# Seven of eight blocks of wo loaded as four neighbouring rows to a lane, with o rearranged to match

## The chip, the cores and the metric

The kernel runs on one core of one Trainium2 chip. The metric is the device time of one execution in microseconds. The core has a matrix engine (PE, with its weight loads shown apart as PEld), a vector engine (DVE), an activation engine (ACT), GpSimd (POOL), and SyncE (SP), which here issues nearly all transfers. Sixteen DMA engines move data between the chip's memory (HBM) and the on-chip memory SBUF; matmuls write to PSUM.

## The reference, cut to what matters

A decode step: four sequences with one token each, width 640, and two branches added to the residual.

```
xn  = layernorm(x)                                # 4 x 640
q   = (xn @ wq)  -> 4 x 32 heads x 128
p   = softmax(q k^T / sqrt(128))                  # over 4096 cached positions
o   = p v        -> 4 x 32 x 128
out = x + o.reshape(4, 4096) @ wo + gmlp(xn)      # wo is 4096 x 640
```

The caches k and v are 4 x 32 x 4096 x 128 in bf16, 128 MiB each. There is one query per head, so every byte of the caches is used once. wo is 4096 x 640 in bf16, 5 MiB. The output is rounded to bf16.

## The kernel before, in words

**Tiles.** The work is cut into NT = 32 steps. Step i is a group hg of HT = 4 heads and one sequence b: `hg, b = divmod(i, 4)`. A step needs one k tile and one v tile of 128 lanes x 16,384 elements, 4 MiB each. A lane holds 128 consecutive positions of one head, so 32 lanes belong to a head, and a lane's 32 KB are contiguous in HBM.

**Loads.** k and v tiles share five buffers (KV_SLOTS); the weights wq, w_in and w_out take three of them first. `pump()` issues the next load from SP (L121) as soon as the tile that held the buffer before has been used. The order is written out in `loads`; twice (EXTRA_K) two k tiles follow each other, and from then on the v part of a step runs one step further behind (`turns`). The last v tile is cut into pieces.

**wo.** There are eight blocks of 512 rows, one for each group of four heads, in one buffer (`wop`, one tile of 128 x 4 x 640). `load_wo(j)` is issued from SP (L155) at the end of step 4j + 2, behind the k and v loads issued by then; block 7 is issued after the loop in four pieces (L153). Row 128 hh + p of a block goes to lane p, part hh. So a lane gets four rows that lie 128 rows apart, 1,280 B each.

**A step.** The order of each engine's instructions is written out by hand. On DVE: the product of k with the query (L397, four quarters), a halving sum of each (L409), the rest of the sum over PE (`sums`, L421) and `row_sums` (L432), then `lane_max` (L441). The maximum is turned on PE (`turn_max`, L446), reduced per head on DVE (`head_max`, L451), spread over lanes on PE (`spread_max`, L462), and used in the exponentials on ACT (L474). These are done in the next step, between the first quarters of its products. `blocks` (L489) and `gather` (L506) form p v on PE, for the step that `turns` names.

**A group.** When the fourth sequence of a group has been through `blocks`, `group_den` sums the exponentials over lanes (L530) and takes the reciprocal (L534), and `group_norm` (L539) writes o_n: 128 lanes (the position in the head) x 4 heads x 4 sequences, bf16. `group_proj` (L548), in the next step after `turn_max`, multiplies it into `out_ps`: eight matmuls, one for each head and half of the 640 columns, with o_n of a head as weights and part hh of wo as moving data. `out_ps` gathers the residual, the gMLP branch and all groups, and is written out at the end.

**PSUM.** qbc_ps, den, mT and nb_ps rotate through one pool, `ps_m`, of two buffers.

Of the kernel before, what the change touches and what calls it, by code (L numbers as in the profile page):

```python
# [9 lines left out]
FP32 = mybir.dt.float32  # L10
BF16 = mybir.dt.bfloat16
ACT = mybir.ActivationFunctionType
ALU = mybir.AluOpType
AX = mybir.AxisListType
# [6 lines left out]
def kernel(  # L21
# [14 lines left out]
    nc = tc.nc  # L36
    P = nc.NUM_PARTITIONS
    Bsz, Sq, D = A_x.shape
# [9 lines left out]
    HT = 4  # L48
    HG = H // HT
    NT = HG * Bsz  # L50
    LN = P // HT
# [12 lines left out]
    const = ctx.enter_context(tc.tile_pool(name="const", bufs=1))  # L64
# [5 lines left out]
    small = ctx.enter_context(tc.tile_pool(name="small", bufs=2))  # L70
# [3 lines left out]
    ps_m = ctx.enter_context(tc.tile_pool(name="ps_m", bufs=2, space=PSUM))  # L74
# [13 lines left out]
    for c0, c1 in ((0, HT), (HT, DC)):  # L88
# [14 lines left out]
        out=w_out_sb[:, 0:NFF, :], in_=B_w_out[0 : NFF * P].rearrange("(p k) n -> p k n", k=NFF)  # L103
# [34 lines left out]
    def pump():  # L138
        while n_loaded[0] < len(loads):
            at = n_loaded[0] + 3 - KV_SLOTS  # L140
            if at >= 0 and occupants[at] not in used:
                return
            load(*loads[n_loaded[0]])
            n_loaded[0] += 1

    wo_v = A_wo.rearrange("(j h p) n -> j p h n", p=P, h=HT)
    wo_tiles = {}

    def load_wo(j):
        wo_tiles[j] = wop.tile([P, HT, D], BF16, name="wo")  # L150
        if j == HG - 1:
            for hh in range(HT):
                nc.sync.dma_start(out=wo_tiles[j][:, hh, :], in_=wo_v[j][:, hh, :])  # L153
            return
        nc.sync.dma_start(out=wo_tiles[j][:], in_=wo_v[j])  # L155

    pump()

# [2 lines left out]
    ident = const.tile([P, P], BF16)  # L161
# [19 lines left out]
        out=sel[:],  # L181
        in_=ident_f[:].rearrange("p (g q) -> p q g", g=CG)[:, 0 : GC * HT, :],
        axis=AX.X,
        op=ALU.add,
    )

    NACC = 2
# [10 lines left out]
    for i in range(NSTAT):  # L198
# [5 lines left out]
        out=rstd[:], in_=mv[:, 1:2], func=ACT.Sqrt, bias=eps_tile[:Bsz], scale=1.0  # L204
# [4 lines left out]
        out=xn_bf[:],  # L209
        in0=x_bf[:],  # L210
# [8 lines left out]
    for c in range(DC):  # L219
        nc.tensor.transpose(  # L220
            out=xnT_ps[:, c, :], in_=xn_v[:, c, :], identity=ident[:Bsz, :Bsz]
# [5 lines left out]
    for h in range(H):  # L227
        for c in range(DC):
            t, i = wq_parts[c]
            nc.tensor.matmul(  # L230
                out=q_ps[:, h, :],
                lhsT=t[:, i, h * Dh : (h + 1) * Dh],
                rhs=xnT[:, c, :],
                start=(c == 0),
                stop=(c == DC - 1),
# [9 lines left out]
    def out_sum(half):  # L245
        return out_ps[OG * half : OG * half + Bsz, :]

    for half in range(2):
        nc.tensor.matmul(
            out=out_sum(half),  # L250
            lhsT=ident[:Bsz, :Bsz],
            rhs=x_bf[:, half * NOH : (half + 1) * NOH],
            start=True,
            stop=False,
# [124 lines left out]
    def stage_q(i):  # L379
        hg, b = divmod(i, Bsz)  # L380
        qb_ps = ps_m.tile([P, Dh], FP32, tag="m", name="qbc_ps")
        for hh in range(HT):
            nc.tensor.matmul(  # L383
                out=qb_ps[hh * LN : (hh + 1) * LN, :],
                lhsT=qT[:, HT * hg + hh, b : b + 1].to_broadcast([P, LN]),
                rhs=ident[:],
                start=True,
                stop=True,
            )
        qbcs[i] = small.tile([P, Dh], BF16, name="qbc", bufs=3)  # L390
        nc.scalar.copy(out=qbcs[i][:], in_=qb_ps[:])  # L391
# [3 lines left out]
    def product(i, q):  # L395
        t = prods[i, q] = prod.tile([P, QC, Dh], BF16, name="prod")
        nc.vector.tensor_tensor(  # L397
            out=t[:],
            in0=k_tiles[i][:, q * QC : (q + 1) * QC, :],
            in1=qbcs[i][:, None, :].to_broadcast([P, QC, Dh]),  # L400
            op=ALU.mult,
        )

    def fold_half(i, q):
        t = prods.pop((i, q))
        half, part = divmod(q, 2)
        if part == 0:
            folds[i, half] = fold.tile([P, HC, HD2], BF16, name="folded")
        nc.vector.tensor_tensor(  # L409
            out=folds[i, half][:, part * QC : (part + 1) * QC, :],  # L410
            in0=t[:, :, 0:HD2],
            in1=t[:, :, HD2:Dh],
            op=ALU.add,
        )

    def sums(i, half):
        t = folds.pop((i, half))
        s = sums_ps[i, half] = ps_s.tile([P, HC, RW], FP32, name="s_ps")
        n = HD2 // RW
        for g in range(n):  # L420
            nc.tensor.matmul(  # L421
                out=s[:],
                lhsT=ident[:],
                rhs=t[:, :, g * RW : (g + 1) * RW],
                start=(g == 0),
                stop=(g == n - 1),
            )
# [72 lines left out]
    def gather(i, stop=True):  # L500
        hg, b = divmod(i, Bsz)
        if b == 0:
            pvs[hg] = ps_pv.tile([P, HT, Bsz], FP32, tag="pv", name="pv")
        pv_sb = blocks_sb.pop(i)
        for k in range(GC):
            nc.tensor.matmul(  # L506
                out=pvs[hg][:, :, b],
                lhsT=pv_sb[:, k * Dh : (k + 1) * Dh],
                rhs=sel[:, k * HT : (k + 1) * HT],
                start=(k == 0),  # L510
                stop=stop and k == GC - 1,
            )
# [13 lines left out]
    gr = {}  # L526
# [10 lines left out]
    def group_norm(hg):  # L537
# [3 lines left out]
        )  # L541
        gr[hg] = o_n

    def group_proj(hg):
        o_n = gr.pop(hg)
        for hh in range(HT):
            for half in range(2):
                nc.tensor.matmul(  # L548
                    out=out_sum(half),
                    lhsT=o_n[:, hh, :],  # L550
                    rhs=wo_tiles[hg][:, hh, half * NOH : (half + 1) * NOH],
                    start=False,
                    stop=(hg == HG - 1 and hh == HT - 1),
                )

    def group(i, fn):
        if 0 <= i < NT and i % Bsz == Bsz - 1:
            fn(i // Bsz)

    def at(i, fn, *args):  # L560
        if 0 <= i < NT:
            fn(i, *args)

    turns = {}
# [8 lines left out]
    with tc.manual_schedule(engines={E.PE, E.DVE, E.Activation, E.SP}):  # L573
        stage_q(0)
        stage_q(1)
        gmlp()
        used.update(occupants[:3])
        pump()
        for i in range(NT):
            j = turns.get(i)  # L580
            product(i, 0)
            fold_half(i, 0)
            at(i - 1, row_sums, 1)
            at(i - 1, lane_max)
            at(i - 1, turn_max)
            group(turns.get(i - 1, -1), group_proj)
            product(i, 1)
            at(i - 1, head_max)
            at(i - 1, spread_max)
            at(i - 1, exps)  # L590
            fold_half(i, 1)
            sums(i, 0)
            product(i, 2)
            if i + 2 < NT:
                stage_q(i + 2)
            fold_half(i, 2)
            due = [] if j is None else [j]
            if i == NT - 1:
                due += range(j + 1, NT - 2)
            for n, jj in enumerate(due):  # L600
                if n:
                    gather(due[n - 1])
                blocks(jj)
                group(jj, group_den)
                used.add(("v", jj))
            row_sums(i, 0)
            product(i, 3)
            fold_half(i, 3)
            if due:
                gather(due[-1])  # L610
            for jj in due:
                group(jj, group_norm)
            sums(i, 1)
            used.add(("k", i))
            pump()
            if i % Bsz == 2 and i // Bsz < HG - 1:
                load_wo(i // Bsz)
        load_wo(HG - 1)
        row_sums(NT - 1, 1)
        lane_max(NT - 1)  # L620
        turn_max(NT - 1)
        head_max(NT - 1)
        spread_max(NT - 1)
        exps(NT - 1)
        blocks(NT - 2)
        group_den(HG - 1)
        gather(NT - 2)
        blocks(NT - 1, 0, V_CUTS[1])
        gather(NT - 1, stop=False)
        for c0, c1 in zip(V_CUTS[1:], V_CUTS[2:]):  # L630
            pairs(NT - 1, c0, c1)
        group_norm(HG - 1)
        group_proj(HG - 1)

        res = work.tile([P, NOH], BF16, name="res")
        out_v = out.flatten_outer_dims()
        r0, r1 = slice(0, Bsz), slice(OG, OG + Bsz)
        nc.scalar.copy(out=res[r0], in_=out_ps[r0])
        nc.vector.tensor_copy(out=res[r1], in_=out_ps[r1])
        nc.scalar.dma_start(out=out_v[:, 0:NOH], in_=res[r0])  # L640
        nc.sync.dma_start(out=out_v[:, NOH:D], in_=res[r1])
# [30 lines left out]
```

## Time and profile before

| | |
|---|---|
| median of 3 runs | 670.0 us (669.78 to 670.29) |
| profiled execution | 669.68 us |
| its span, first to last instruction | 667.9 us |
| DVE busy | 506.7 us |
| PE busy | 347.9 us |
| moved by DMA | 282.63 MB in 14,663 packets, of which 5,548 are under 2 KB |
| wo, issue to landing (median of 7) | 44.7 us |
| k, issue to landing (median of 32) | 43.3 us |

The span is the part of the execution that the trace covers; the 1.8 us around it belong to the execution's own time. Busy time is per engine, and engines work beside each other. A DMA packet is one contiguous piece that one DMA engine moves; the time from issue to landing includes the time that a transfer stands in the queue behind others.

### The profile page before, as it was taken

What the parts mean: (1) busy time and instruction counts of PE and PEld (TensorE: products, weight loads), DVE (VectorE), ACT (ScalarE), POOL (GpSimd) and SP (SyncE); (2) the same over time, 40 slices, a digit from 0 to 9 for tenths busy, and PEclk for the clock granted to TensorE, in tenths of its full rate; (3) what the DMA queues carried; (4) which work ended last, traced back from release to release, by engine and by line L of the source; (5) the groups of instructions that cost most, each with busy time, mean ns of one, the idle gap of its engine ahead of it and who ended that gap; (6) DMA issues with size and microseconds to landing.
All of it is one profiled execution on the core that took longest, in us unless ns stands there. A gap on an engine that the chain in (4) does not pass through costs nothing.

```text
span 667.9 us, 5968 instructions
## 1 busy us (share of the span) xinstructions
PE 347.9 (52%) x2425; PEld 154.7 (23%) x2425; DVE 506.7 (76%) x435; ACT 113.0 (17%) x361; POOL 2.7 (0%) x13
## 2 busy tenths in 40 slices
PE   1627554535557345663346654455564556546575
PEld 0502221212222122221112221122222112222133
DVE  1299897867789677787777698776787899876961
ACT  0202111101111101111101111111111111110122
POOL 1000000000000000000000000000000000000000
PEclk9997766788766678775786866788766667786677
DMA  9999999999999999999999999999999999999996
GB/s 373 418 440 433 419 433 436 420 435 426 429 426 430 433 430 429 424 431 432 434 421 432 423 434 435 428 426 429 424 435 434 421 430 432 429 422 433 432 422 257
DMA packets 14663, 282.63 MB, mean 423 GB/s; under 512 B 1344, under 2 KB 5548, under 8 KB 5932
## 3 DMA queue, kind: packets, MB, share of 16 engines
q1 hardware_dynamic: 14616, 282.25, 99.1%
q8 instruction: 19, 0.31, 0.2%
q14 instruction: 8, 0.07, 0.0%
q10 hardware_dynamic: 20, 0.01, 0.0%
HBM read 282.24 MB, written 0.01 MB: 423 GB/s over the span
## 4 chain that ended last, share of the span: by engine, by line
DMA 68%; DVE 21%; PE 8%; SPq 1%; issue 1%; DVEq 0%
DMA k_nat<-in_A_k_cache_dram 63%; DVE prod L397 13%; PE s_ps L421 7%; DVE folded L409 5%; DMA v_nat<-in_A_v_cache_dram 5%; DVE s_sb L432 2%; PE pv_acc L489 1%; SPq L121 1%; DVE m L441 1%; DVE nm L451 0%; PE out_ps L548 0%; PE qbc_ps L383 0%; SPq L90 0%; SPq L102 0%; PE den L530 0%
## 5 line engine op out<-in xcount | busy, mean ns | idle before, releaser
L397 DVE TENSOR_TENSOR prod<-k_nat,qbc 128x4096 bf16<-128x4096 bf16 x128 | 292.7, 2287 | 91.4 <-DMA k_nat<-in_A_k_cache_dram 89.9
L421 PE MATMUL s_ps<-folded,ident 128*128 128x512 bf16 x512 | 186.9, 531 | 64.7 <-DVE folded L409 64.6
L409 DVE TENSOR_TENSOR folded<-prod 128x2048 bf16<-128x2048 bf16 x128 | 156.1, 1220 | 3.3
L421 PEld LDWEIGHTS <-ident 128*128 128x128 bf16 x512 | 64.9, 128 | 152.4 <-issue 135.3
L446 PE MATMUL mT<-ident_f,m 128*1 128x128 f32 x32 | 11.0, 344 | 154.8 <-DVE m L441 154.8
L474 ACT ACTIVATE pm<-s_sb,nb 32x128 bf16<-32x128 f32 x128 | 73.9, 578 | 2.6
L470 ACT COPY nb<-nb_ps 128x4 f32<-128x4 f32 x32 | 5.2, 162 | 394.9 <-PE nb_ps L462 394.9
L489 PE MATMUL pv_acc<-v_nat,pm 128*16 128x512 bf16 x1008 | 71.7, 434 | 0.2 <-DMA v_nat<-in_A_v_cache_dram 0.2
L432 DVE TENSOR_REDUCE s_sb<-s_ps 128x64 f32<-128x512 f32 x64 | 43.5, 680 | 7.8 <-PE s_ps L421 5.4
L462 PE MATMUL nb_ps<-nm,scale_row 1*128 1x4 f32 x64 | 18.2, 353 | 56.2 <-DVE nm L451 56.2
L506 PE MATMUL pv<-sel,pv_sb 128*128 128x4 f32 x256 | 34.4, 258 | 19.5 <-ACT pv_sb L497 19.5
L446 PEld LDWEIGHTS mT<-ident_f,m 128*1 128x1 f32 x32 | 2.5, 79 | 173.1 <-DVE m L441 141.8
L506 PEld LDWEIGHTS pv<-sel,pv_sb 128*128 128x128 f32 x256 | 31.6, 195 | 32.3 <-ACT pv_sb L497 32.3
L489 PEld LDWEIGHTS <-pm 128*16 128x16 bf16 x1008 | 26.6, 102 | 32.6 <-issue 17.2
L474 ACT ACTIVATION_READ_ACCUMULATOR pm<-s_sb,nb 32x1 f32 x128 | 32.2, 251 | 0.0
L462 PEld LDWEIGHTS nb_ps<-nm,scale_row 1*128 1x128 f32 x64 | 15.5, 299 | 66.7 <-DVE nm L451 59.8
L497 ACT COPY pv_sb<-pv_acc 128x512 f32<-128x512 f32 x32 | 18.7, 585 | 61.4 <-PE pv_acc L489 61.4
L391 ACT CAST qbc<-qbc_ps 128x128 bf16<-128x128 f32 x32 | 8.4, 265 | 80.0 <-PE qbc_ps L383 80.0
L534 DVE RECIPROCAL rden<-den 128x16 f32<-128x16 f32 x8 | 2.1, 258 | 21.9 <-PE den L530 21.9
L238 DVE CAST qT<-q_ps 128x128 bf16<-128x128 f32 x1 | 0.3, 292 | 15.1 <-PE q_ps L230 15.1
L230 PE MATMUL q_ps<-xnT,wq 128*128 128x4 bf16 x160 | 4.6, 167 | 10.5 <-DMA wq<-in_A_wq_dram 10.5
L441 DVE TENSOR_REDUCE m<-s_sb 128x1 f32<-128x128 f32 x32 | 9.2, 287 | 1.1
(76 smaller groups left out, 79.2 us busy)
## 6 DMA issues: line engine op xcount, KB each, us to landing
k_nat<-in_A_k_cache_dram SPq DMA_DIRECT2D x32, 4096.0 KB, 43.3
v_nat<-in_A_v_cache_dram SPq DMA_DIRECT2D x31, 4096.0 KB, 36.6
wo<-in_A_wo_dram SPq DMA_DIRECT2D x7, 640.0 KB, 44.7
wq<-in_A_wq_dram SPq DMA_DIRECT2D x1, 4096.0 KB, 12.7
w_sb<-in_B_w_in_dram SPq DMA_DIRECT2D x1, 2160.0 KB, 19.5
v_nat<-in_A_v_cache_dram SPq DMA_DIRECT2D x1, 2048.0 KB
wq<-in_A_wq_dram SPq DMA_DIRECT2D x1, 1024.0 KB, 14.8
v_nat<-in_A_v_cache_dram SPq DMA_DIRECT2D x1, 1024.0 KB
```

The costliest lines, as they stand in the source:

```text
L391: nc.scalar.copy(out=qbcs[i][:], in_=qb_ps[:])
L397: nc.vector.tensor_tensor(out=t[:], in0=k_tiles[i][:, q * QC : (q + 1) * QC, :], in1=qbcs[i][:, None, :].to_broadcast([P, QC, Dh]), op=ALU ...
L409: nc.vector.tensor_tensor(out=folds[i, half][:, part * QC : (part + 1) * QC, :], in0=t[:, :, 0:HD2], in1=t[:, :, HD2:Dh], op=ALU.add,)
L421: nc.tensor.matmul(out=s[:], lhsT=ident[:], rhs=t[:, :, g * RW : (g + 1) * RW], start=(g == 0), stop=(g == n - 1),)
L432: nc.vector.tensor_reduce(out=scores[i][:, half * HC : (half + 1) * HC], in_=sums_ps.pop((i, half))[:], axis=AX.X, op=ALU.add,)
L441: nc.vector.tensor_reduce(out=m1[:], in_=scores[i][:], axis=AX.X, op=ALU.max)
L446: nc.tensor.transpose(out=mT[:], in_=maxes[i][:], identity=ident_f[:])
L462: nc.tensor.matmul(out=nb_ps[:], lhsT=scale_row[:], rhs=maxes[i][:], start=True, stop=True)
L474: nc.scalar.activation(out=pm[ps, :, hh], in_=s_sb[ps, :], func=ACT.Exp, bias=nb[ps, hh : hh + 1], scale=scale_qk, accum_out=a[ps, hh, b : ...
L489: nc.tensor.matmul(out=pv_acc[g * LN : g * LN + GC * HT, :], lhsT=pm[:, c : c + GC, :].rearrange("p c h -> p (c h)"), rhs=v_nat[:, c : c + ...
L497: nc.scalar.copy(out=pv_sb[:], in_=pv_acc[:])
L506: nc.tensor.matmul(out=pvs[hg][:, :, b], lhsT=pv_sb[:, k * Dh : (k + 1) * Dh], rhs=sel[:, k * HT : (k + 1) * HT], start=(k == 0), stop=sto ...
```

## The change

The first seven blocks of wo are loaded so that lane p gets the rows 4p to 4p + 3 of the block, which are neighbours in HBM: 5,120 contiguous bytes. Block 7 stays as it was. Lane p of a block then belongs to head p // 32, and its part r to position 4 (p mod 32) + r of that head, so o must stand in the same order before it can be multiplied in.

Two steps do that. `group_turn` runs on PE after `sums(i, 1)`: four matmuls, one for each r, whose weights `spread[:, r]` are columns 4m + r of the identity, once for each of four heads. They put o_n's position 4m + r on lane 32h + m, for all four heads of o_n, into a PSUM tile of 128 x 4 x 4 x 4 from the pool `ps_m`. `group_pick` runs on DVE in the next step, between `turn_max` and `group_proj`: a multiplication with the mask `hmask`, which keeps on each lane the one head that belongs there, and a sum over the four heads, which writes o_r in bf16. `group_proj` is the same code; its index hh now counts the part r, and its weights come from o_r. The constants `spread` and `hmask` are made once at the start.

For group 7 neither step is issued, since it is projected after the loop.

```
-    wo_v = A_wo.rearrange("(j h p) n -> j p h n", p=P, h=HT)
+    wo_r = A_wo.rearrange("(j p r) n -> j p (r n)", p=P, r=HT)
+    wo_h = A_wo.rearrange("(j h p) n -> j p h n", p=P, h=HT)
...
         if j == HG - 1:
             for hh in range(HT):
-                nc.sync.dma_start(out=wo_tiles[j][:, hh, :], in_=wo_v[j][:, hh, :])
+                nc.sync.dma_start(out=wo_tiles[j][:, hh, :], in_=wo_h[j][:, hh, :])
             return
-        nc.sync.dma_start(out=wo_tiles[j][:], in_=wo_v[j])
+        nc.sync.dma_start(out=wo_tiles[j][:].rearrange("p r n -> p (r n)"), in_=wo_r[j])
...
+    hmask = const.tile([P, HT], FP32)
+    nc.vector.memset(hmask[:], 0.0)
+    for hh in range(HT):
+        nc.vector.memset(hmask[hh * LN : (hh + 1) * LN, hh : hh + 1], 1.0)
+    spread = const.tile([P, HT, HT, LN], BF16)
+    nc.vector.tensor_copy(
+        out=spread[:],
+        in_=ident[:].rearrange("p (m r) -> p r m", r=HT)[:, :, None, :].to_broadcast(
+            [P, HT, HT, LN]
+        ),
+    )
...
+    def group_turn(hg):
+        ps = ps_m.tile([P, HT, HT, Bsz], FP32, tag="m", name="o_ps")
+        for r in range(HT):
+            nc.tensor.matmul(
+                out=ps[:, r, :, :],
+                lhsT=spread[:, r, :, :].rearrange("p h m -> p (h m)"),
+                rhs=gr[hg][:].rearrange("p h b -> p (h b)"),
+                start=True,
+                stop=True,
+            )
+        gr[hg] = ps
+
+    def group_pick(hg):
+        own = small.tile([P, HT, HT, Bsz], FP32, name="own")
+        nc.vector.tensor_tensor(
+            out=own[:],
+            in0=gr[hg][:],
+            in1=hmask[:, None, :, None].to_broadcast([P, HT, HT, Bsz]),
+            op=ALU.mult,
+        )
+        o_r = small.tile([P, HT, Bsz], BF16, name="o_r")
+        with nc.allow_low_precision("one of the four is the value, the others are zeros"):
+            nc.vector.tensor_reduce(
+                out=o_r[:],
+                in_=own[:].rearrange("p r h b -> p r b h"),
+                axis=AX.X,
+                op=ALU.add,
+            )
+        gr[hg] = o_r
...
             at(i - 1, turn_max)
+            group(turns.get(i - 1, -1), group_pick)
             group(turns.get(i - 1, -1), group_proj)
...
             sums(i, 1)
+            for jj in due:
+                group(jj, group_turn)
```

## The prediction

> **What bounds the kernel now.** I read the page's busy shares and its 40 slices first, then the DMA queues, then the chain that ended last.
>
> ```profile
> span 667.9 us, 5968 instructions
> ...
> PE 347.9 (52%) x2425; PEld 154.7 (23%) x2425; DVE 506.7 (76%) x435; ACT 113.0 (17%) x361; POOL 2.7 (0%) x13
> ...
> GB/s 373 418 440 433 419 433 436 420 435 426 429 426 430 433 430 429 424 431 432 434 421 432 423 434 435 428 426 429 424 435 434 421 430 432 429 422 433 432 422 257
> ...
> q1 hardware_dynamic: 14616, 282.25, 99.1%
> ...
> DMA 68%; DVE 21%; PE 8%; SPq 1%; issue 1%; DVEq 0%
> ...
> L397 DVE TENSOR_TENSOR prod<-k_nat,qbc 128x4096 bf16<-128x4096 bf16 x128 | 292.7, 2287 | 91.4 <-DMA k_nat<-in_A_k_cache_dram 89.9
> ...
> k_nat<-in_A_k_cache_dram SPq DMA_DIRECT2D x32, 4096.0 KB, 43.3
> ```
>
> SP's queue holds the 16 DMA engines for 99.1% of the span, while DVE, the busiest engine, is busy for 76% and spends 89.9 us waiting for k. A k tile lands 43.3 us after its issue, and 4 MiB at 423 GB/s take 9.9 us, so about four tiles lie queued. Whatever shortens the packets' own time should therefore shorten the run, and whatever makes an engine a little later should not. The DVE and PE shares of the chain are the walk back from one issue to the work that freed its slot; they are no proof that DVE binds.
>
> Next, what wo's packets cost. The DMA view of two short stretches, the first with wo block 0 passing (119.6 to 124.0 us), the second with k and v alone (124 to 128 us); a queue's columns are packets, MB and share of 16 engines:
>
> ```profile
> DMA packets 578, 1.77 MB, mean 402 GB/s; under 512 B 32, under 2 KB 544, under 8 KB 544
> ...
> q1 hardware_dynamic: 578, 1.77, 102.8%
> ```
> ```profile
> DMA packets 51, 1.67 MB, mean 418 GB/s; under 512 B 0, under 2 KB 0, under 8 KB 0
> ...
> q1 hardware_dynamic: 51, 1.67, 97.1%
> ```
>
> The second gives a k or v packet: 0.971 x 4 us x 16 engines = 62.1 us for 51 packets of 32,768 B, 1.218 us each. The first holds 1.028 x 4.4 x 16 = 72.4 us. In it are 544 - 32 = 512 rows of wo, 1,280 B each, 34 large packets (41.4 us) and 32 tiny ones (9 ns each by the packet records, 0.3 us). That leaves 30.7 us for 512 rows: 60 ns a row. The packet records of the trace, which hold each packet's size and time, say it more exactly: 58.4 ns a row over the eight wo blocks, 161.8 ns for the 4,096 B packets of the last v pieces, 311.8 ns for their 8,192 B packets, 1,222 ns for 32,768 B. At the rate of the large packets a row would take 47.7 ns; so a packet bears about 11 ns that does not grow with its size.
>
> **The change, part by part.**
>
> *Seven wo loads.* Before, a block is 512 packets, 32 to an engine. After, if a lane's four rows travel as one packet, it is 128 packets of 5,120 B, 8 to an engine. No packet of this size is in the trace. From below it is bounded by the rate of the large packets, 5,120 x 1.222 / 32,768 = 191 ns; from above by four rows as now, 4 x 58.4 = 234 ns; nothing suggests dearer, since every larger packet moves its bytes at a higher rate than 1,280 B do. I take the line between the nearest rows, 161.8 + (311.8 - 161.8) x 1,024 / 4,096 = 199 ns. The saving is 234 - 199 = 35 ns for four rows, x 8 = 0.28 us per engine and block, x 7 = **1.9 us**. The ends give 7 x 8 x 43 ns = 2.4 us, and 0; with the coarser 60 ns and 191 ns, 2.7 us. An independent check: the slices in which blocks 0 to 6 pass (seven, with the mean of two neighbours for block 1) average 425 GB/s, and the others of the steady part about 431; 6/431 of 16.7 us is 0.23 us lost per block. That is near the 0.34 us (32 x 10.7 ns) that rows cost over the large packets' rate, of which the change should return 0.28.
>
> A rule speaks against this. The Trainium skill, "DMA: Bandwidth & Descriptors", section "Specifications", sets the least transfer for line rate at 512 B, which makes 1,280 B good enough and the gain nothing; its section "Why small descriptors are slow (HBM only)" charges about 3 cycles per packet on a 32 B bus, by which four rows take 4 x 43 = 172 cycles against 163, and at the 850 MHz of its table the estimate is 10.6 ns x 56 = 0.6 us. The row disagrees: 58.4 ns against 47.7 is a fixed part three times as large. I go by the row.
>
> *SP and the rest of the queue.* The same number of issues in the same places (0.43 us each now). The single wo buffer is freed by the projection of the block before: 127.3 to 128.3 us for block 0, next issue at 159.0. Half a microsecond later is nothing there. Block 7 and the tail from the last v landing (663.0) to the end keep their code, so they only come earlier.
>
> *TensorE, `group_turn`, seven times.* Four weight loads of 128x128 bf16 and four matmuls of 16 columns. The nearest rows are L276 (70 pairs, 128x4, in 4.0 us at the start, 57 ns a pair) and L506 (eight f32 pairs in 1.06 us): 0.25 to 1.0 us a group. It waits for o_n, which DVE makes right after the fold that `sums(i, 1)` ahead of it needs anyway. Behind it on PE stands `turn_max`, which needs row_sums and lane_max, 0.68 + 0.29 us of DVE after the sums end. At 120.83 us the sums run 3.47 us to 124.3; the transpose comes at 127.08 with 2.77 us of idle PE before it. So it lies in that idle time. Where DVE runs without a break (522 to 570 us) the cover is about 1 us, and the worst is a few tenths.
>
> *DVE, `group_pick`, seven times.* A multiply 128x64 f32 out of PSUM: L285 has 218 ns for 128x56, so 0.23 us. A reduction from 64 to 16: L180 has exactly 128x16 from 128x64, 249 ns. In sum 0.48 us a group, 3.4 us in all. It waits for `group_turn`, done by 125.3 us, before lane_max ends at 126.9. Behind it: product(i, 1), then head_max, spread_max and the exponentials, all some 0.5 us later; and `group_proj` on PE, which now waits for o_r. The projection takes 1.06 us, and PE idled 1.03 us after it for nm, which moves as well. DVE's cover is its wait for the next k (1.6 us before 122.46, 3.6 us before 102.94). If this cover is gone, the price is up to 3.4 us, and then it must pass through the queue too, which holds four tiles. The thinnest place is 519 to 552 us: one tile is issued there while 33 us pass, 3.3 tiles' time, so about two tiles (20 us) remain. Half a microsecond doesn't show.
>
> *PSUM, start, code.* The order in the two-buffer pool becomes qbc_ps, den, o_ps, mT, nb_ps; nb_ps takes o_ps's buffer, freed by the pick, and must wait for nm behind it on DVE anyway. The constants (five memsets, one copy of 128x512) cost at most 5 x 0.17 + 0.49 = 1.3 us by the rows of L166 and L178. DVE idles 15.13 us before qT; even ahead of everything they would move xnT from 5.1 to 6.4 us, and q_ps starts at 13.5 when wq lands. Some 80 instructions join 5,968 whose fetching is 0.2% of the DMA share. All this I put at nothing.
>
> **Sum.** 669.68 us, the profiled execution (span 667.9 and 1.8 around it), less 1.9 gives 667.8. That execution lies 0.3 us under the median of the runs, 670.0; against the median I forecast **668.1 us**, 0.28% less. A measurement of this kernel can tell about 0.2%, 1.34 us, from no change, so my forecast clears that by only half a microsecond.
>
> **Rivals.**
>
> *Nothing to be had from packets.* The rows' low rate may be made up by other engines: the stretch 120 to 124 us, a little narrower than mine, moves 424 GB/s with wo in it, hardly less than the mean of 423. Or the load still goes as rows of 1,280 B, because the tile has dimensions for them. Against the first: those shares count above 100%, and per share the wo stretch moves 402/1.028 = 391 against 418/0.971 = 430 GB/s; the slices show the loss too. Against the second: wq, four contiguous rows of 8 KB to a lane, went as packets of 32,768 B. The time is then 669.4 to 670.0, say 669.8. It also covers a 5,120 B packet above 210 ns, by which the gain is at most 1.34 us.
>
> *The pick comes onto the path.* Place: the unbroken DVE stretch from 522 to 570 us and the seven picks. Price: 3.4 us of DVE, and with a wait of about 0.3 us each for the turn, 5.5 us; less 1.9, that is +1.5 to +3.6: 671.5 to 673.6, say 672.5. It decides from the point where SP's queue runs dry, when a tile's time from issue to landing falls towards the 9.9 us of one transfer. For it: DVE has no gap in those 48 us. Against it: 43 us to landing, 430 GB/s in those slices, and 89.9 us of DVE idle elsewhere.
>
> **How the numbers follow.** Forecast (a saving of over 1.34 us) 0.70; no gain from packets 0.23; the pick on the path 0.07. So faster 0.70, within 0.2% 0.23, slower 0.07. The range runs from 2.8 us of saving (the bound of 2.7 and the spread of the runs) to none: 667.2 to 670.0, which leaves out most of the last rival and the edges.
>
> **What would show it.** The page's packet count falls by 7 x 384 = 2,688, and those under 2 KB from 5,548 to about 2,860. A stretch with wo passing should hold 128 packets of about 199 ns in place of 512. The share of q1 stays at 99%, the span falls by 1.9. DVE's busy time rises by some 3.4 + 0.5 to 1.3 us, its wait for k by less than it did or falls. I am wrong if the packet count falls and the span does not (first rival), if k's time to landing collapses or a slice drops below 420 GB/s (second), or if 5,120 B take 234 ns.

## The result, and the profile after

The changed kernel takes 664.64 us (median of 5 runs, 664.44 to 664.98) against 670.0 us: a ratio of 0.992, 95% interval 0.991 to 0.993. That is 5.4 us less, where 1.9 were forecast, and below the stated range. Here is the page of the profiled execution (664.64 us, span 662.8), the same lines as before:

```profile
span 662.8 us, 6037 instructions
...
PE 352.1 (53%) x2453; PEld 157.5 (24%) x2453; DVE 510.5 (77%) x455; ACT 113.1 (17%) x361; POOL 2.7 (0%) x13
...
GB/s 374 424 443 427 427 440 430 433 432 427 436 428 435 438 427 430 433 430 441 432 425 440 425 435 439 427 434 433 426 439 431 430 434 430 434 431 432 437 420 268
DMA packets 11975, 282.63 MB, mean 426 GB/s; under 512 B 1344, under 2 KB 1964, under 8 KB 3244
...
q1 hardware_dynamic: 11928, 282.25, 99.0%
...
DMA 63%; DVE 24%; PE 10%; ACT 1%; issue 1%; SPq 1%; DVEq 0%; ACTq 0%
...
L411 DVE TENSOR_TENSOR prod<-k_nat,qbc 128x4096 bf16<-128x4096 bf16 x128 | 292.7, 2287 | 80.6 <-DMA k_nat<-in_A_k_cache_dram 79.1
...
k_nat<-in_A_k_cache_dram SPq DMA_DIRECT2D x32, 4096.0 KB, 43.0
```

The packet count fell by 14,663 - 11,975 = 2,688, as the merging of four rows asks for. The queue is as full as before (99.0%), k still takes 43 us to landing, and the same bytes pass at a higher mean rate, 426 against 423 GB/s, with more in most of the slices and not only in those with wo. That is the first sign that wo's packets are not the whole story. A stretch with k and v alone, 40 to 115 us, tells it. The kernel before and then the changed one, in the DMA view:

```profile
DMA packets 1114, 32.25 MB, mean 430 GB/s; under 512 B 128, under 2 KB 128, under 8 KB 128
...
q1 hardware_dynamic: 1111, 32.21, 100.0%
```
```profile
DMA packets 1120, 32.42 MB, mean 432 GB/s; under 512 B 128, under 2 KB 128, under 8 KB 128
...
q1 hardware_dynamic: 1116, 32.38, 100.1%
```

No wo passes here, and still 5 more large packets get through in the same 75 us. So the 4 MiB tiles themselves move faster, by about half a per cent. The packet records, which the trace holds beside these views with each packet's size and time, put numbers to it. There are 8,192 packets of 32,768 B, 8,064 of k and v and 128 of wq. One took 1,222.0 ns on average before and 1,216.2 after; 8,070 of them now take exactly 1,213 ns, where 94 did before, 91 of these being wq's. Summed and divided by the 16 engines, packet time fell by 5.6 us: 3.0 from the 32,768 B packets, 2.1 from the seven wo blocks (13.1 to 11.0), and 0.5 from all the others. The time fell by 5.4.

What could change k and v packets, when neither their source nor their order was touched? The two new constants take 1,056 bytes of each lane and were allocated ahead of the k and v buffers. Those buffers, and all that lies behind them, moved up: from byte 24,800 of a lane to 25,856. The first is 224 more than a multiple of 256; the second is a multiple of 256. (The profile shows no addresses: these come from the allocation of the tiles, and the distances between the runs below follow from their edits.)

### The profile page after: what moved, and what is told of

It is laid out like the page before. It is cut to its first block, busy times and chain, and to the rows that moved or that the text cites. A ratio compares the mean times of both kernels' runs of the same rounds, so it can differ in the third digit from the quotient of the medians.

```text
span 662.8 us, 6037 instructions
## 1 busy us (share of the span) xinstructions
PE 352.1 (53%) x2453; PEld 157.5 (24%) x2453; DVE 510.5 (77%) x455; ACT 113.1 (17%) x361; POOL 2.7 (0%) x13
## 2 busy tenths in 40 slices
DMA packets 11975, 282.63 MB, mean 426 GB/s; under 512 B 1344, under 2 KB 1964, under 8 KB 3244
## 4 chain that ended last, share of the span: by engine, by line
DMA 63%; DVE 24%; PE 10%; ACT 1%; issue 1%; SPq 1%; DVEq 0%; ACTq 0%
DMA k_nat<-in_A_k_cache_dram 63%; DVE prod L411 14%; PE s_ps L435 7%; DVE folded L423 6%; DVE s_sb L446 3%; PE pv_acc L503 2%; PE pv L520 1%; DVE m L455 1%; DVE nm L465 0%; ACT pv_sb L511 0%; ACT pm L488 0%; SPq L121 0%; PE pv L532 0%; PE out_ps L593 0%; SPq L102 0%
## 5 line engine op out<-in xcount | busy, mean ns | idle before, releaser
L411 DVE TENSOR_TENSOR prod<-k_nat,qbc 128x4096 bf16<-128x4096 bf16 x128 | 292.7, 2287 | 80.6 <-DMA k_nat<-in_A_k_cache_dram 79.1
L476 PE MATMUL nb_ps<-nm,scale_row 1*128 1x4 f32 x64 | 18.4, 355 | 58.3 <-DVE nm L465 58.3
L244 PE MATMUL q_ps<-xnT,wq 128*128 128x4 bf16 x160 | 4.6, 166 | 10.6 <-DMA wq<-in_A_wq_dram 10.6
```

The lines of the kernel that those rows point to most:

```text
L411: nc.vector.tensor_tensor(out=t[:], in0=k_tiles[i][:, q * QC : (q + 1) * QC, :], in1=qbcs[i][:, None, :].to_broadcast([P, QC, Dh]), op=ALU ...
L476: nc.tensor.matmul(out=nb_ps[:], lhsT=scale_row[:], rhs=maxes[i][:], start=True, stop=True)
```

## The experiments

The theory ADDRESS says that the place of the buffers is worth what wasn't forecast. The rival PACKETS says that it all comes from wo's packets. Unless told otherwise, an edit is made to the kernel before, and the ratio is to that kernel on the same chip (669.9 to 670.05 us).

**e1: only the address.**

```
     qT = const.tile([P, H, Bsz], BF16)
+    pad = const.tile([P, 8], FP32)
+    nc.gpsimd.memset(pad[:], 0.0)
```

> The kernel before with one unused constant of 32 bytes a lane, made after qT, so that the k and v buffers and wo start at a multiple of 256 bytes (24,832) as they do after the change (25,856), and not at 24,800. wo is still loaded as rows of 1,280 B. Theory ADDRESS (the change's new constants moved the buffers, and DMA writes to them got cheaper): 32,768 B packets fall from a mean of 1,222 ns to about 1,216, rows from 58.4 to about 55, and the time is 670.0 - 4.0 = 666.0 us. Rival PACKETS (all 5.4 us come from wo's packets being fewer, which also disturb k and v less): no change, 670.0 us.

Measured: 666.16 us, ratio 0.994 (0.9925 to 0.9952). The 32,768 B packets take 1,216.2 ns, the rows of 1,280 B 55.1 ns. The same stretch of 40 to 115 us in e1 reads as in the changed kernel:

```profile
DMA packets 1119, 32.39 MB, mean 432 GB/s; under 512 B 128, under 2 KB 128, under 8 KB 128
...
q1 hardware_dynamic: 1115, 32.34, 100.0%
```

Thirty-two unused bytes are worth 3.9 us. By the packet records the packets' time, divided by the 16 engines, falls by 4.2 us: 3.0 from the 32,768 B packets, 0.9 from the rows of 1,280 B and 0.4 from the others. PACKETS falls.

**e3: only the packets.** The changed kernel, with 224 unused bytes (`pad` of 56 elements), so that the buffers again stand 224 past a multiple of 256.

> The changed kernel with an unused constant of 224 bytes a lane, so that the buffers start at 26,080, which is 224 more than a multiple of 256, as in the kernel before (24,800). wo goes as packets of 5,120 B, o is turned. Theory ADDRESS: 32,768 B packets are back at 1,222 ns, and only the merged packets are left of the gain, 670.0 - 1.9 = 668.1 us, the time that was forecast. Rival PACKETS: no change to the changed kernel, 664.6 us.

Measured: 668.08 us, ratio 0.997 (0.996 to 0.998); 1,221.4 ns a large packet, 199.0 ns a packet of 5,120 B. Its stretch of 40 to 115 us:

```profile
DMA packets 1109, 32.09 MB, mean 428 GB/s; under 512 B 128, under 2 KB 128, under 8 KB 128
...
q1 hardware_dynamic: 1106, 32.05, 99.5%
```

So the change without its move of the buffers is worth what was forecast for it. The four cases side by side, as medians; the last column is what merging the rows saves, the last line what the address saves:

| time, us | rows of 1,280 B | packets of 5,120 B | merging |
|---|---|---|---|
| buffers 224 past a multiple of 256 | 670.05 (before, on the chip of e1 and e3) | 668.08 (e3) | 2.0 |
| buffers at a multiple of 256 | 666.16 (e1) | 664.64 (changed) | 1.5 |
| address | 3.9 | 3.4 | |

**e11: a control.** The same 32 bytes and the same memset, in a pool behind all others, so that no buffer moves.

> A control: the kernel before with the same unused constant of 32 bytes and its memset, put behind all other buffers, so that nothing else moves. Theory ADDRESS: 670.0 us, 1,222 ns. If the constant or its instruction did something by itself: 666.1 us, as with the constant ahead of the buffers.

Measured: 670.12 us, ratio 1.000 (0.999 to 1.001), 1,221.9 ns. The constant by itself does nothing.

**e2, e5, e10: which addresses.** `pad` of 96, 160 and 64 bytes puts the buffers 64, 128 and 32 past a multiple of 256.

> The kernel before with an unused constant of 96 bytes a lane: the buffers start at 24,896, a multiple of 64 but not of 128. Theory ADDRESS with 64 bytes as what counts: 666.0 us, as with 32 bytes. Theory ADDRESS with 128 or 256 bytes as what counts: 670.0 us. Rival PACKETS: 670.0 us.

> The kernel before with an unused constant of 160 bytes a lane: the buffers start at 24,960, a multiple of 128 but not of 256. If a start at a multiple of 128 is enough: as with a multiple of 256, 666.1 us, and 32,768 B packets of 1,216 ns. If it takes a multiple of 256: about 669.7 us and 1,221 ns, as 24,896 (64 over) gave.

> The kernel before with an unused constant of 64 bytes a lane: the buffers start at 24,864, 32 over a multiple of 256. If the loss grows with the distance from the multiple of 256 (the Trainium skill, page DMA: Bandwidth & Descriptors, section How a descriptor splits into AXI transactions, counts the beats from the boundary below the start: one of 32 bytes here, seven in the kernel before), that page's estimate is 1,214 ns a packet and a time near 666.5 us. If any start off the multiple costs about the same, as 64, 128 and 224 over did: 1,221 ns and 669 to 670 us.

Measured, in the order of the distance: 32 past, 669.88 us (ratio 1.000, 0.999 to 1.001) and 1,221.7 ns; 64 past, 669.65 us (0.999, 0.998 to 1.000) and 1,220.8 ns; 128 past, 669.14 us (0.999, 0.998 to 1.000) and 1,220.6 ns. A multiple of 64 or of 128 isn't enough, and 32 bytes off the mark cost all of it. The loss doesn't grow with the distance. An estimate from the beats in the Trainium skill, "DMA: Bandwidth & Descriptors", section "How a descriptor splits into AXI transactions", has the boundary that counts here, 256 bytes, but not the size: by those beats 32 past should lose a seventh of what 224 past loses, and it loses the same. That section speaks of what a transaction reads; the runs here moved only the place that is written.

**e9 and e12: is there a better multiple?** The changed kernel with `pad` of 256 bytes (buffers at 26,112), and as it is, on the same chip.

> The changed kernel with an unused constant of 256 bytes a lane: the buffers start at 26,112, a multiple of 512. All fast kernels so far (24,832 and 25,856) start at 256 over a multiple of 1,024. If a multiple of 256 is what counts: no change, 664.7 us and packets of 1,213 ns. If 256 over 1,024 was a lucky place: slower, up to 668.1 us. If a multiple of 512 is better still: under 664.3 us.

> The changed kernel once more, on the chip of the run with 256 bytes added, for a comparison of the two: 664.6 us.

Measured: 664.93 us (664.85 to 666.39; ratio 0.993, 0.992 to 0.995) and 664.65 us (0.992, 0.991 to 0.993); 1,216.4 and 1,216.2 ns. Two of e9's five runs took 666.4 us; the packets of one of them are those of the 1,216.4 ns, so that isn't the address. A multiple of 256 is what counts among the places tried, and no tried version is faster than the changed kernel. Told as shifts of the buffers against the kernel before: by 32, 1,056 and 1,312 bytes, each 32 more than a multiple of 256, the packets are fast; by 0, 64, 96, 160 and 1,280 they aren't.

**e6, e7: whose address.** A pool of 224 or 32 bytes between the k and v buffers and wo moves wo, prod and folded by themselves.

```
+    gap = ctx.enter_context(tc.tile_pool(name="gap", bufs=1))
     wop = ctx.enter_context(tc.tile_pool(name="wop", bufs=1))
...
+    gap_t = gap.tile([P, 56], FP32)
+    nc.gpsimd.memset(gap_t[:], 0.0)
```

(e6, which also has e1's `pad`; e7 has 8 elements in the gap and no `pad`.)

> The kernel before with k and v at a multiple of 256 and everything behind them (wo, prod, folded) at 224 over one. Theory DESTINATION (a packet's own write address sets its time): 32,768 B packets 1,216 ns, rows of wo 58.4 ns, time 666.2 + 8 x 32 x 3.3 ns = 667.0 us. Rival COMPUTE (reads and writes of DVE at odd addresses in prod and folded slow the transfers): both packets slow, 670.0 us.

> The other way round: k and v at 224 over a multiple of 256 as before, wo, prod and folded at a multiple of 256. Theory DESTINATION: 32,768 B packets 1,222 ns, rows of wo 55 ns, time 670.0 - 0.8 = 669.2 us. Rival COMPUTE: both packets fast, 666.2 us.

Measured: e6 665.82 us (ratio 0.994, 0.993 to 0.995), large packets 1,216.7 ns, rows 55.2 ns. e7 668.31 us (0.998, 0.997 to 0.999), 1,220.5 and 55.1 ns. COMPUTE is out: prod and folded off the multiple cost nothing in e6, and put right in e7 they don't bring the fast packets back. But DESTINATION fails in part too. In e6 wo stands off the multiple and its rows are fast, so a packet's own address doesn't settle its time. In e7 some 23% of the large packets take 1,213 ns, though the buffers stand where they stood before: after wo blocks, whole tiles come through at 1,213 ns. And in the kernel before, wq's packets, loaded into the same buffers in the first 20 us, took 1,213 ns at the median. In e7 fast and slow are thus stretches of the stream of packets, about two tiles long after each wo block, and not properties of one buffer. That isn't so at every address: in e5 24% of the large packets take 1,213 ns, and they are spread over nearly all tiles.

**e8: five addresses in one kernel.** Each k and v buffer is 32 bytes longer (`SLOT + 16`), on top of e1.

> The kernel before with the first buffer at a multiple of 256 and each buffer 32 bytes longer, so that the five buffers of k and v start at 0, 32, 64, 96 and 128 over a multiple of 256, and wo at 160 over. Theory DESTINATION: two fifths of the 32,768 B packets (0 and 128 over) at 1,213 ns if 128 is enough, one fifth if it takes 256, the others at 1,214 to 1,224 ns; rows of wo 58 ns. Time between 666.2 and 670, about 668.5 us. If only the first buffer's address counted or the pools behind it: all packets alike.

One run: 668.03 us; 1,219.5 ns on average, 39% of the large packets at 1,213 ns; rows 57.7 ns. The time lies between the ends, as it should. The 39% don't show that 128 past is a good place, since e5 has only 24% there. Nor can they be put down to single buffers: of every fifth tile in order of start, which use one buffer, one series has 70 to 80% of its packets at 1,213 ns in its first four tiles and 0 to 20% in its last six. The run is inconclusive beyond that.

**e4: are the turn and the pick hidden?**

```
-            for jj in due:
-                group(jj, group_turn)
...
-            group(turns.get(i - 1, -1), group_pick)
```

(in the changed kernel)

> The changed kernel without the turn and the pick: o_n is multiplied with the rearranged wo as it is, so the projection of seven groups is not the reference's; the constants stay, so no buffer moves. If the added PE and DVE work is hidden behind the queue: 664.6 us, within 0.5. If the pick is on the path in part: faster, down to 661 us.

Measured: 664.96 us, ratio 0.993 (0.991 to 0.994), on top of the changed kernel's. So leaving out the turn and the pick saves nothing: both are hidden.

**e13, e14: do engine accesses take part?** DVE's products and halving sums are cut to one of 32 columns (`QC` columns become 1 in both), once with the buffers at 24,800 and once with e1's `pad`.

> The kernel before, buffers at 24,800, with DVE's products and halving sums over one of 32 columns of each quarter (the rest of the scores is left out, so the output is not the reference's); transfers and their destinations are the same. If reads and writes of DVE at these addresses slow the transfers: 32,768 B packets at 1,213 to 1,216 ns and a time near 666 us. If the transfers alone make the slower packets: 1,222 ns and near 669.5 us.

> The same omission with the 32 bytes ahead of the buffers, which start at 24,832. 1,216 ns and near 666 us under both theories; the difference to its partner is what the address is worth without DVE's big instructions: 0 to 1 us if DVE is part of it, 3 to 4 us if it isn't.

Measured: e13 670.76 us (ratio 1.002, 1.001 to 1.003) and 1,222.3 ns; e14 667.24 us (0.996, 0.995 to 0.997) and 1,216.3 ns. The busy shares of e13:

```profile
span 668.9 us, 5967 instructions
...
PE 406.6 (61%) x2425; PEld 173.3 (26%) x2425; DVE 119.6 (18%) x435; ACT 112.7 (17%) x361; POOL 9.6 (1%) x15
...
q1 hardware_dynamic: 14616, 282.25, 99.0%
```

DVE is down from 506.7 to 119.6 us and the time hasn't fallen at all (why it is 0.85 us longer is open); the address is still worth 3.5 us. So DVE's big reads and writes aren't needed for the slower packets; the accesses of the other engines were left as they were. e13 is also the plainest sign of what bounds this kernel.

## Why the prediction was wrong, point by point

*The bound: right.* SP's queue holds the DMA engines for 98.8 to 99.1% of the span in every variant, and most of the packet time that was saved showed in the time: 5.4 of 5.6 us in the changed kernel, 3.9 of 4.2 in e1. e13 removes three quarters of DVE's work for nothing.

*Seven wo loads: right.* A packet of 5,120 B was taken at 199 ns; it takes 199.0 in e3, where the address is as before, and the time is 668.08 us against the 668.1 forecast. So this part of the forecast held for the reason given; that the times agree to the last digit is luck, as e3's interval runs from 667.4 to 668.9 us. In the changed kernel it takes 196.0. Its DMA view with block 0 passing, 119 to 123 us:

```profile
DMA packets 192, 1.70 MB, mean 426 GB/s; under 512 B 32, under 2 KB 32, under 8 KB 160
...
q1 hardware_dynamic: 192, 1.70, 100.3%
```

128 merged packets, 32 tiny ones and 32 large ones: 1.003 x 4 x 16 = 64.2 us, less 32 x 1.213 and 0.3, is 25.1 us, 196 ns each. A large packet's rate would make 190 ns.

*The weight given to the row over the rules of the Trainium skill ("DMA: Bandwidth & Descriptors", sections "Specifications" and "Why small descriptors are slow (HBM only)"): right.* Four rows took 34 to 35 ns more than one packet at the old address (4 x 58.4 - 199) and 24 more at the new one (4 x 55.1 - 196). By the first rule, as the prediction read it, that would be nothing; the estimate from the second was 10.6 ns. But part of the 11 ns that each row seemed to bear whatever its size came with the address: at the new one it is 55.1 - 47.4 = 7.7 ns, where 47.4 is a row's share of a packet of 1,213 ns.

*PE and DVE: right, at nothing.* The groups of the changed kernel (count, busy us, mean ns of one, idle before):

```profile
L562 PE MATMUL o_ps<-o_n,spread 128*128 128x16 bf16 x28 | 2.1, 186 | 0.0
L581 DVE TENSOR_REDUCE o_r<-own 128x16 bf16<-128x64 f32 x7 | 1.8, 261 | 0.2
L573 DVE TENSOR_TENSOR own<-o_ps,hmask 128x64 f32<-128x64 f32 x7 | 1.5, 213 | 0.0
L194 DVE COPY spread<-ident 128x512 bf16<-128x512 bf16 x1 | 0.4, 409 | 0.0
```

The pick takes 0.474 us where 0.48 was worked out, and DVE hardly waits for it (0.2 us in all). The timeline around block 0's group shows why: start, duration, engine, operation:

```profile
121.34 3.57 PE L435 MATMUL s_ps<-folded,ident 128*128 128x512 bf16 x8 [2.92 <-DVE folded L423]
...
124.70 0.30 PE L562 MATMUL o_ps<-o_n,spread 128*128 128x16 bf16 x4
125.06 0.68 DVE L446 TENSOR_REDUCE s_sb<-s_ps 128x64 f32<-128x512 f32 x1
125.78 0.29 DVE L455 TENSOR_REDUCE m<-s_sb 128x1 f32<-128x128 f32 x1
125.98 0.21 DVE L573 TENSOR_TENSOR own<-o_ps,hmask 128x64 f32<-128x64 f32 x1
```

The turn fits behind the sums and is done a microsecond before the pick. The price of 3.3 us on DVE is paid out of its wait for k, which falls from 89.9 to 79.1 us. In e4, the changed kernel without the turn and the pick, that wait is 84.6 us:

```profile
L411 DVE TENSOR_TENSOR prod<-k_nat,qbc 128x4096 bf16<-128x4096 bf16 x128 | 292.7, 2287 | 86.1 <-DMA k_nat<-in_A_k_cache_dram 84.6
```

So about half of the fall comes with the turn and the pick, and the other half was there without them.

*The constants: the step that failed.* "The constants (five memsets, one copy of 128x512) cost at most 5 x 0.17 + 0.49 = 1.3 us ... All this I put at nothing." Their instructions do cost nothing (409 ns for the copy, hidden). But only the instructions were priced, and not the bytes. The bytes move every buffer allocated after them, and the time of the packets of k and v hung on where those buffers start. The term that was put at nothing measures 3.4 to 3.9 us of run time: 3.4 from e3 to the changed kernel, 3.9 from the kernel before to e1. Of the 5.6 us of packet time saved, the 3.0 on the 32,768 B packets are there, and most of the 0.5 on the others. The prediction's bounds for unknown costs covered the merged packet, and left out that packets which the change doesn't touch might change. None of the signs that it named for being wrong covers this, and none of them came.

*The rivals.* The packets' gain was there, as e3 shows with nothing else changed; the pick never came onto the path. Neither rival had anything to do with what happened. No chance was set aside for a gain outside wo's packets, and so the range ended at 667.2 us.

*The counts.* The packet count fell by 2,688 as forecast. But the packets under 2 KB fell to 1,964, and not to about 2,860: the prediction took 2,688 off 5,548, while all 3,584 rows of the seven blocks leave that class.

Of the chain: in the kernel before, its last part was a transfer (v, landing at 663.0). In the changed kernel it is engine work from 609 us on, DMA's share falling from 68% to 63%. The transfers' end and the last step's computation now lie close together: in e4, which takes the same time, the last part of the chain is a v transfer again (DMA 67%). That a further saving in the queue would bring less than its own size at the end is argued from this, not shown.

## What to carry to other kernels

A change that adds a constant also moves every buffer allocated behind it, as the 1,056 bytes did here; where transfers are the bound, look at the start addresses of the large destinations in both versions before putting a price on anything else. Two cheap kernels separate the two effects: the old one with an unused tile of the right size, and the new one with its buffers put back; a third, with the tile where it moves nothing, is the control. Here 32 unused bytes were worth twice the change that was meant.

## What the runs showed of the hardware that was not expected

Loads from HBM in packets of 32,768 B took 1,213 ns each, almost without exception, when the k and v buffers began at a multiple of 256 bytes in a lane, and mostly 1,214 to 1,224 ns when they began 32, 64, 128 or 224 bytes past one (1,213 ns for 1, 6, 24 and 1% of them, in this order). It is half a per cent of a packet, and here 3.4 to 3.9 us of a run.

| k, v past a multiple of 256 | wo past it | 32,768 B, ns | 1,280 B, ns | kernel, us |
|---|---|---|---|---|
| 224 | 224 | 1,222.0 | 58.4 | before, 670.0 |
| 32 | 32 | 1,221.7 | 58.4 | e10, 669.9 |
| 64 | 64 | 1,220.8 | 58.3 | e2, 669.7 |
| 128 | 128 | 1,220.6 | 58.0 | e5, 669.1 |
| 224 | 0 | 1,220.5 | 55.1 | e7, 668.3 |
| 0 | 224 | 1,216.7 | 55.2 | e6, 665.8 |
| 0 | 0 | 1,216.2 | 55.1 | e1, 666.2 |

Why it is so stays open. It doesn't grow with the distance from the multiple (e10), it doesn't need DVE's big products and sums (e13, e14), and a packet's own address doesn't settle it (e6, e7, and wq at the start of the kernel before). No run here shows what does.
